# A new memory layout for an FNet block with a gate: x, P, Q and W2 on the 256-byte grid, first tokens staged in the combining buffer

## The chip, the cores and the metric

The kernel runs on one core of one Trainium2 chip. The metric is the device time of one execution in microseconds (us). The kernel before took 714.79 us (median of 3 runs, 714.57 to 714.8). All data are float32; TensorE is fed in the format fp32r (float32 rounded for one pass), so that each product is made from several passes, as told below.

## The reference

With x of 2048 tokens by 512 features (one batch), two 2048 x 2048 and two 512 x 512 DFT matrices, w1 of 512 x 1792 and w2 of 1792 x 512:

```python
xn = layernorm(x)                                   # over features, eps 1e-5
a  = einsum("bsd,ed->bse", xn, dft_hid_re)
b  = einsum("bsd,ed->bse", xn, dft_hid_im)
y  = einsum("ts,bse->bte", dft_seq_re, a) - einsum("ts,bse->bte", dft_seq_im, b)
h  = relu(xn @ w1 + b1) ** 2
out = x + y * silu(h @ w2 + b2)
```

## The kernel before, in words

**Three passes.** Every float32 operand is split into a high part (ScalarE copies it with rounding, `split_hi` L68) and a low part (VectorE subtracts, `split_lo` L71). A product is HI·HI + HI·LO + LO·HI (`PASSES`), three matmuls into one PSUM bank.

**Seven products for eight.** Most products are 2 x 2 block products in seven multiplications (`PRODUCTS`, `ORDER`), with sums of blocks of the one operand (`sums_a`), of the other (`sums_b`) and of the results (`combine`). `A11` to `S4` and `B11` to `T4` name the blocks and sums. A matmul of this kind has 128 x 128 weights and 256 moving columns; each weight load precedes its matmul and runs beside the one before it.

**The stages, in the order of the span** (times in us of the profiled execution):

1. 0 to 112: x is normalised, split and laid down in eight buffers `XC[j]` of 7 blocks x (HI, LO) x 256 floats. The first two chunks (c = 0, 1) of the sequence DFT are done without the seven-product scheme (`products`, L340; 512 moving columns from g1a/g1b, weights from XC). In chunk 1 the sums of x and the splits of the 512 x 512 DFT matrices (`wd_split`, into wd0 and wd1) are made beside it.
2. 112 to 414: chunks c = 2 to 7. Each has 8 steps j; a step is 7 products x 6 matmuls (`mm`, L287): moving operand g0/g1 (`moving`, the split sums of the raw DFT rows that `load_c` brings into `r`), weights `XC[j]`. At a chunk's end the results are combined in `e` and split into P and Q (`pq`, tiles pq00 to pq11). Behind steps 1 and 2 of the next chunk follow the two calls of `stage2` (L273), which multiply P and Q with the feature DFT: 24 passes each, weights from pq, 512 moving columns from wd0/wd1; some of the passes are split into two halves of 256 columns. The result y goes to DRAM. W1 and W2 are also prepared here (`make_w`), written to DRAM.
3. 414 to 564: hidden layer, 28 units (4 token groups c x 7 pairs of 256 hidden features p), 42 matmuls each (L527): weights W1[p], moving operand xT[c, q], the transposed normalised tokens. The two `stage2` calls of chunk 7 follow unit 0. Results are squared and go to DRAM (`HD`).
4. 564 to 706: output product, again 28 units of 42 matmuls (L581): weights are the reloaded, summed and split hidden features g (`operand`, `ready`), moving operand W2[p]. Then silu, times y, plus x, and out. In the last token group the products of the last three p are done product by product, so that the end can start early.

**What sets the order.** Stage 1 for c = 0, and everything from the hidden units on, are written out by hand (`manual_schedule`): `plan` and `go` name what is issued ahead of and behind each unit: `m` loads the rows of mean and 1/deviation, `x` a half token group (`xt_half`), `w` a late W2 block, `h` a step of `operand` (reload, sums, split), `l` a load of a W2 block (`load_w2`, L480). The rest, stages 1 (c = 1) and 2, is ordered by the planner from its own time estimates; DMA loads go through SP's queue.

**Buffers.** SBUF tiles with one tag share a place in turn. The eight x buffers xc0 to xc7 are tiles of 14336 bytes per partition each. They are given new contents later: xc0, xc1 take xT of even token groups and then W2's p = 0, 1; xc2 to xc7 take W1's p = 0 to 5, xc4 to xc6 then g, xc7, xc2, xc3 W2's p = 2, 3, 4. wd0 and wd1 take xT of odd groups and then W2's p = 5, 6. W1's p = 6 lies in g0b and g1b. The first group's tokens are staged, at the steps j = 2 and 3 of chunk 7, in new tiles with the tags xc2 and xc3 (`stage{q}`, L675).

**Remainders.** Tiles lie one behind the other in the order in which their tags are first used, each rounded up to 32 bytes. Counting the sizes gives each tile's address modulo 256. The eight x buffers begin at 3840 and are 56 x 256 bytes long: remainder 0. Behind them the tile `gap` (L113) takes 192 bytes, and the tiles that follow (pq, r, g0, g1, wd, t, e, sx) all have multiples of 256 bytes, or are made such by what precedes them: remainder 192. Blocks inside a tile are multiples of 512 bytes apart, so that an operand has its tile's remainder.

Of the kernel before, what the change touches and what calls it, by code (L numbers as in the profile page):

```python
# [12 lines left out]
P = 128  # L13
# [7 lines left out]
WARM = 8, 5  # L21
PLAIN = 2
# [39 lines left out]
def fnet_gated_kernel(ctx, tc, x, xt, ct, wd, w1, w2, b1, b2, out):  # L62
# [201 lines left out]
    def stage2(c, t, tag="bc"):  # L264
        ps = bank(tag, f"yps{c}_{t}")[:, 0]
        for m in range(2):
            for k in range(ND):
                w = (k % 2) * CW + t * P
                for a_, b_ in PASSES:
                    last = (a_, b_) == (LO, HI) and (m, k) == (1, ND - 1)  # L270
                    pair = (a_, b_) != (HI, HI) and (m, k) in ((0, 1), (1, ND - 1))[t:]
                    for s in (slice(0, 256), slice(256, 512)) if pair else (slice(0, 512),):
                        nc.tensor.matmul(ps[:, s], PQ[c, m, k // 2][:, a_, w:w + P], WD[m, k][:, b_, s],  # L273
                                         start=(m, k) == (0, 0) and (a_, b_) == (HI, HI), stop=last,
                                         skip_group_check=True)
# [200 lines left out]
    W2_HOME = "xc0", "xc1", "xc7", "xc2", "xc3", "wd0", "wd1"  # L476

    def load_w2(p):
        t = W2[p] = buf(W2_HOME[p], [P, 2, 7, 256], f"w2_{p}", F32R)
        nc.sync.dma_start(t.bitcast(F32), W2D[p])  # L480
# [62 lines left out]
    def operand(n, c, p):  # L543
# [18 lines left out]
        g = ready[c, p] = buf(("xc4", "xc5", "xc6")[n % 3], [P, 2, 7, 256], f"g{c}_{p}", F32R)  # L562
# [86 lines left out]
    for c, j in steps:  # L649
# [88 lines left out]
    plan(c, 4, ["l2", "h2"], ["h1"])  # L738
    plan(c, 5, ["h4"], ["h1"])
# [174 lines left out]
```

## Time and profile before

| | |
|---|---|
| time, median of 3 runs | 714.79 us |
| profiled execution: time / span | 714.79 / 713.0 us |
| 0 to 112.24 (layer norm, chunks 0 and 1) | 112.24 us |
| 112.24 to 414.02 (six chunks, twelve stage 2 calls) | 301.78 us |
| 414.02 to 564.45 (hidden units, two stage 2 calls) | 150.43 us |
| 564.45 to 669.43 (output product, groups 0 to 2) | 104.98 us |
| 669.43 to 713.0 (last group, end) | 43.57 us |

The stage borders are the starts of PE's first matmul of a stage. PE is TensorE's matmul unit, PEld its weight load, DVE VectorE, ACT ScalarE, POOL GpSimd, SP the queue that issues most DMAs. In a row of groups, `x42` counts instructions, and "us" is the time from the start of the first to the end of the last. Matmuls overlap by a part of their length, so that the pace of PE is the time from start to start, and not the duration of one (about 280 ns for 256 columns). PEclk is the clock that the throttle granted, 1.00 being full speed. In a window row each engine has its busy time and, in brackets, its number of instructions.

### The profile page before, as it was taken

The numbers are of one execution on the slowest core, as the hardware profiler recorded it, in microseconds if no ns is written. First come the engines' busy times: TensorE is split into PE (matmuls) and PEld (weight loads), VectorE is DVE, ScalarE is ACT, GpSimd is POOL, SyncE is SP. The second block draws the span as 40 slices with busy tenths as digits, with TensorE's granted clock in tenths as the row PEclk, the third lists the DMA queues.
The fourth block names the chain that finished last, engine by engine and source line by source line (L and its number), as shares of the span: only waits on it lengthen the run. The fifth ranks groups of instructions, "written<-read, shape, count | busy, mean of one in ns | idle before, by whom it ended". The sixth has DMA issues, their size and how long they took to land.

```text
span 713.0 us, 12788 instructions
## 1 busy us (share of the span) xinstructions
PE 699.1 (98%) x5197; PEld 662.0 (93%) x5197; DVE 584.8 (82%) x886; ACT 347.1 (49%) x475; POOL 5.2 (1%) x8
## 2 busy tenths in 40 slices
PE   8999999999999999999999999999999999999996
PEld 5778788999999999999999999999999999999995
DVE  7999654779598698797795955999988989989895
ACT  4437333444453544444442424777667764454541
POOL 0000000000000000000000000000000000101000
PEclk9999999999999999999999999999999999999999
DMA  9622531634564653844825669966725996667643
GB/s 325 221 89 90 170 117 39 221 95 143 200 216 133 218 190 125 281 148 151 296 90 160 227 234 350 351 241 207 265 105 190 357 397 196 184 214 201 218 149 113
DMA packets 55020, 141.11 MB, mean 198 GB/s; under 512 B 5041, under 2 KB 21681, under 8 KB 53681
## 3 DMA queue, kind: packets, MB, share of 16 engines
q1 hardware_dynamic: 49840, 124.56, 51.3%
q10 hardware_dynamic: 4032, 14.68, 5.3%
q0 software_dynamic: 1088, 1.05, 1.0%
q8 instruction: 41, 0.67, 0.4%
q14 instruction: 19, 0.15, 0.1%
HBM read 97.00 MB, written 43.27 MB: 197 GB/s over the span
## 4 chain that ended last, share of the span: by engine, by line
PE 83%; DVE 13%; issue 2%; ACT 1%; DMA 0%; DVEq 0%; ACTq 0%
PE m_b L287 24%; PE yps L273 12%; PE m_b_o L581 10%; PE hps L527 9%; PE hps_b L527 5%; PE m_bb L287 5%; PE m_ba L287 5%; DVE g L71 3%; PE pq_b L340 3%; PE hps_ba L527 3%; DVE xc L71 2%; PE m_bc_o L581 1%; DVE bn L128 1%; PE m_ba_o L581 1%; PE m_bb_o L581 1%
## 5 line engine op out<-in xcount | busy, mean ns | idle before, releaser
L287 PE MATMUL m_b<-g,xc 128*128 128x256 f32 x1440 | 179.2, 280 | 0.0
L287 PEld LDWEIGHTS m_b<-g,xc 128*128 128x128 f32 x1440 | 173.3, 189 | 0.4
L71 DVE TENSOR_TENSOR g<-r,g 128x768 fp32r<-128x768 f32 (+2 forms) x65 | 65.5, 1007 | 42.0 <-ACT g L68 41.7
L68 ACT ACTIVATE g<-r 128x768 fp32r<-128x768 f32 (+2 forms) x65 | 57.4, 886 | 84.7 <-PE m_b L287 43.9
L273 PE MATMUL yps<-wd,pq 128*128 128x512 f32 (+1 forms) x432 | 93.2, 366 | 0.0
L273 PEld LDWEIGHTS yps<-wd,pq 128*128 128x128 f32 x432 | 75.8, 188 | 13.4
L581 PE MATMUL m_b_o<-w,g 128*128 128x256 f32 x630 | 78.5, 281 | 0.5 <-ACT m_b_o L574 0.5
L581 PEld LDWEIGHTS m_b_o<-w,g 128*128 128x128 f32 x630 | 76.0, 191 | 0.7 <-ACT m_b_o L574 0.7
L340 PE MATMUL pq_b<-g,xc 128*128 128x512 f32 x240 | 64.7, 399 | 3.9 <-ACT xc L68 2.1
L71 DVE TENSOR_TENSOR g<-t,g 128x1024 fp32r<-128x1024 f32 x48 | 58.6, 1222 | 12.1 <-ACT g L68 12.0
L527 PE MATMUL hps<-xT,w 128*128 128x256 f32 x504 | 61.9, 282 | 0.0
L527 PEld LDWEIGHTS hps<-xT,w 128*128 128x128 f32 x504 | 60.8, 190 | 0.0
L340 PEld LDWEIGHTS pq_b<-g,xc 128*128 128x128 f32 x240 | 43.9, 188 | 17.5 <-ACT xc L68 3.6
L68 ACT ACTIVATE g<-t 128x1024 fp32r<-128x1024 f32 x48 | 50.3, 1048 | 17.0 <-PE m_ba L287 6.5
L538 ACT ACTIVATE h<-h,b1s 128x512 f32<-128x512 f32 x56 | 37.3, 715 | 17.6 <-DVE h L237 17.5
L68 ACT ACTIVATE g<-hr 128x768 fp32r<-128x768 f32 (+1 forms) x28 | 35.5, 1269 | 20.9 <-PE m_ba_o L581 5.3
L71 DVE TENSOR_TENSOR g<-hr,g 128x768 fp32r<-128x768 f32 (+1 forms) x28 | 41.6, 1485 | 2.3 <-ACT g L68 2.2
L287 PE MATMUL m_bb<-g,xc 128*128 128x256 f32 x288 | 42.7, 280 | 0.0
L287 PE MATMUL m_ba<-g,xc 128*128 128x256 f32 x288 | 42.5, 280 | 0.0
L287 PEld LDWEIGHTS m_bb<-g,xc 128*128 128x128 f32 x288 | 37.8, 189 | 0.3
L287 PEld LDWEIGHTS m_ba<-g,xc 128*128 128x128 f32 x288 | 37.5, 189 | 0.0
L196 DVE TENSOR_TENSOR t<-r 128x512 f32<-128x512 f32 x48 | 32.9, 685 | 5.2 <-DMA r<-in_ct 5.0
(172 smaller groups left out, 1004.0 us busy)
## 6 DMA issues: line engine op xcount, KB each, us to landing
r<-in_ct SPq DMA_DIRECT2D x63, 512.0 KB, 3.7
hd<-h ACTq DMA_DIRECT2D x28, 512.0 KB, 4.5
hr<-hd SPq DMA_DIRECT2D x28, 512.0 KB, 4.6
w1d<-w0g SPq DMA_DIRECT2D x21, 512.0 KB, 3.5
w<-w1d SPq DMA_DIRECT2D x6, 1792.0 KB, 9.2
w<-w2d SPq DMA_DIRECT2D x4, 1792.0 KB, 12.0
y<-ysb SPq DMA_DIRECT2D x16, 256.0 KB, 3.2
fin<-y SPq DMA_DIRECT2D x16, 256.0 KB, 5.2
```

The lines of the kernel that those rows point to most:

```text
L68: nc.scalar.activation(hi, src, AF.Copy)
L71: return nc.vector.tensor_tensor(lo, src, hi.bitcast(F32), op=ALU.subtract)
L128: nc.vector.bn_stats(bn, t[:, h])
L196: nc.vector.tensor_tensor(t[:, 0:2], r[:, 0:1].to_broadcast([P, 2, 256]), r[:, 1:3], op=ALU.add)
L273: nc.tensor.matmul(ps[:, s], PQ[c, m, k // 2][:, a_, w:w + P], WD[m, k][:, b_, s], start=(m, k) == (0, 0) and (a_, b_) == (HI, HI), stop=last,
L287: nc.tensor.matmul(ps[:, d * CW:(d + 1) * CW], w[:, a_, d * P:(d + 1) * P], mv(b_), start=first and d == 0 and (a_, b_) == (HI, HI), stop= ...
L340: nc.tensor.matmul(accs[c][k], w, g[:, b_, 2 * h:2 * h + 2], start=j == 0 and h == 0 and (a_, b_) == (HI, HI), stop=j == NJ - 1 and h == 1 ...
L527: nc.tensor.matmul(product(ms, k), W1[p][a][:, a_, q * P:(q + 1) * P], xT[c, q][:, b_, b], start=share not in first, stop=q == 1 and (a_, ...
L538: nc.scalar.activation(x_[:, s], x_[:, s], AF.Relu, bias=b1s[:, f:f + 1])
L581: nc.tensor.matmul(m[:, k * 256:(k + 1) * 256], g[:, a_, a, k * P:(k + 1) * P], W2[p][:, b_, b], start=p == 0 and k == 0 and (a_, b_) == ( ...
```

## The change

`LINE` is 16 floats, 64 bytes.

- The order of the tiles is written down: xc0, xc1, the four pq tiles, wd0, wd1, then one tile `block` for the other six x buffers with 64 spare bytes, then the small `stats_t`, g0a, g1a, g0b, g1b, b1s and eps, and the rest as it comes. The tile `gap` and the small tiles laid down ahead of time (`few`) are gone.
- x buffer j from 2 to 7 is a slice of `block`, from the top down (`sixth`): the x data with offset 0, W1's p = 0 to 5 and g at the same places with an offset of 64 bytes, W2's p = 2, 3, 4 in the places of j = 5, 6, 7 with offset 0. A slice with the offset overlaps by 64 bytes with the one above it.
- By the same count, xc0, xc1, pq, wd and `block` now have the remainder 0; g0 and g1 192; r 32; t, e and sx 64.

| product (line) | moving, weights before | moving, weights after |
|---|---|---|
| chunks 0, 1 (L340), chunks 2 to 7 (L287) | 192, 0 | 192, 0 |
| stage 2 (L273) | 192, 192 | 0, 0 |
| hidden, p < 6, even / odd c (L527) | 0, 0 / 192, 0 | 0, 64 |
| hidden, p = 6, even / odd c | 0, 192 / 192, 192 | 0, 192 |
| output, p = 0 to 4 / 5, 6 (L581) | 0, 0 / 192, 0 | 0, 64 |

- `stage2` writes its passes as a list of 24 and splits other ones in halves. Before, in the first call of a chunk passes 4, 5, 22, 23 (counted from 0) were split, in the second 22 and 23. Now pass 23 is split in every call but the last of all, and in the first call of chunks before 7 passes 4 and 5 too; in the last call of all pass 1 is split and its second half is done at the very end.
- The first group's tokens are staged in `e` (the rows, and the raw first half), in an r and in t tiles, in steps: load at j = 2 and 4, the rest at j = 3 and 6. W1's first loads stay at j = 4 to 7.
- The load of W2's p = 2 (`l2`) is issued at unit (3, 5) of the hidden layer instead of (3, 4).

```diff
+LINE = 16
...
-    small = {tag: [buf(tag, [P, n], f"{tag}_{i}", bufs=3) for i in range(3)] for tag, n in (("bn", 12), ("sm", 4))}
...
-    XC = [buf(f"xc{j}", [P, 7, 2, 256], f"xc{j}", F32R) for j in range(NJ)]
-
-    pool.tile([P, 48], F32, name="gap")
+    for tag, n in [("xc0", 3584), ("xc1", 3584)] + [(f"pq{m}", 1024) for m in ("00", "01", "10", "11")] \
+            + [("wd0", 4096), ("wd1", 4096)]:
+        buf(tag, [P, n], f"place_{tag}")
+    block = pool.tile([P, 6 * 3584 + LINE], F32R, name="block")
+    stats_t = pool.tile([P, 2 * NS], F32, name="stats_t")
+    for tag, n in (("g0a", 1536), ("g1a", 2048), ("g0b", 1536), ("g1b", 2048)):
+        buf(tag, [P, n], f"place_{tag}")
...
+    def sixth(j, a, on=LINE):
+
+        v = block[:, (7 - j) * 3584 + on:][:, 0:3584]
+        return v.rearrange("p (a b n) -> p a b n", a=a, n=256)
+
+    XC = [buf(f"xc{j}", [P, 7, 2, 256], f"xc{j}", F32R) if j < 2 else sixth(j, 7, 0) for j in range(NJ)]
...
     def stage2(c, t, tag="bc"):
         ps = bank(tag, f"yps{c}_{t}")[:, 0]
...
+        whole, one, two = slice(0, 512), slice(0, 256), slice(256, 512)
+        todo = [(m, k, a_, b_, whole) for m in range(2) for k in range(ND) for a_, b_ in PASSES]
+
+        def divide(n):
+            todo[n:n + 1] = [(*todo[n][:4], half) for half in (one, two)]
+
+        if (c, t) == (NC - 1, 1):
+            divide(1)
+            todo.append(todo.pop(2))
+        else:
+            divide(23)
+        if c < NC - 1 and t == 0:
+            divide(5)
+            divide(4)
...
-            t = buf(f"xc{2 + (p + 2) % 6}", [P, 2, 7, 256], f"w1_{p}", F32R)
+            t = sixth(2 + p, 2)
...
-    W2_HOME = "xc0", "xc1", "xc7", "xc2", "xc3", "wd0", "wd1"
+    W2_HOME = "xc0", "xc1", 5, 6, 7, "wd0", "wd1"
...
-        t = W2[p] = buf(W2_HOME[p], [P, 2, 7, 256], f"w2_{p}", F32R)
+        to = W2_HOME[p]
+        t = W2[p] = sixth(to, 2, 0) if p in (2, 3, 4) else buf(to, [P, 2, 7, 256], f"w2_{p}", F32R)
...
-        g = ready[c, p] = buf(("xc4", "xc5", "xc6")[n % 3], [P, 2, 7, 256], f"g{c}_{p}", F32R)
+        g = ready[c, p] = sixth(2 + n % 3, 2)
...
-            if j in (2, 3):
-                q = j - 2
-                t = buf(f"xc{2 + q}", [P, 3, 4, 256], f"stage{q}")
-                if q == 0:
-                    load_rows(0, t[:, 0])
-                list(xt_half(0, q, lambda k: t[:, 1 if k == "r" else 2]))
-            elif j > 3:
+            if j == 2:
+                e = buf("e", [P, 8, 256], "rows0")
+                load_rows(0, e[:, 0:4])
+            if j in (2, 4):
+                first = xt_half(0, j // 2 - 1, lambda k: e[:, 4:8] if (j, k) == (2, "r") else
+                                buf(k, [P, 4, 256], f"x{k}0", bufs=3 if k == "r" else 2))
+                next(first)
+            if j in (3, 6):
+                list(first)
+            if j > 3:
                 load_w1(j - 4)
...
-    plan(c, 4, ["l2", "h2"], ["h1"])
-    plan(c, 5, ["h4"], ["h1"])
+    plan(c, 4, ["h2"], ["h1"])
+    plan(c, 5, ["l2", "h4"], ["h1"])
```

More of the change, by code (lines that the diff above doesn't have):

```diff
@@ L79, in fnet_gated_kernel @@
     dram = ctx.enter_context(tc.tile_pool(name="dram", bufs=1, space=bass.MemoryType.DRAM))
-    b1s = pool.tile([P, NF], F32, name="b1s")
     b2s = pool.tile([P, D], F32, name="b2s")
-    eps = pool.tile([P, 1], F32, name="eps")
     stats = pool.tile([P, 2, 2, NJ], F32, name="stats")
-    stats_t = pool.tile([P, 2 * NS], F32, name="stats_t")
     rows = dram.tile([2 * NS, P], F32, name="rows")
     Y = [dram.tile([TC, D], F32, name=f"y{t}") for t in range(NTC)]
-    nc.vector.memset(eps, EPS)
     def bank(tag, name):
@@ L96, in buf @@
         return pool.tile(shape, dtype, tag=tag, bufs=bufs, name=name)
-    small = {tag: [buf(tag, [P, n], f"{tag}_{i}", bufs=3) for i in range(3)] for tag, n in (("bn", 12), ("sm", 4))}
-    def few(tag, n, name):
-        return small[tag].pop(0) if small[tag] else buf(tag, [P, n], name, bufs=3)
     def bcast(src, n):
@@ L108, in halves @@
         return ap.rearrange("p (a b) -> p a b", a=2)
-    XC = [buf(f"xc{j}", [P, 7, 2, 256], f"xc{j}", F32R) for j in range(NJ)]
-    pool.tile([P, 48], F32, name="gap")
+    for tag, n in [("xc0", 3584), ("xc1", 3584)] + [(f"pq{m}", 1024) for m in ("00", "01", "10", "11")] \
[5 more added lines that the diff above has]
+        buf(tag, [P, n], f"place_{tag}")
+    b1s = pool.tile([P, NF], F32, name="b1s")
+    eps = pool.tile([P, 1], F32, name="eps")
+    nc.vector.memset(eps, EPS)
+    def sixth(j, a, on=LINE):
+        v = block[:, (7 - j) * 3584 + on:][:, 0:3584]
+        return v.rearrange("p (a b n) -> p a b n", a=a, n=256)
+    XC = [buf(f"xc{j}", [P, 7, 2, 256], f"xc{j}", F32R) if j < 2 else sixth(j, 7, 0) for j in range(NJ)]
     xr, xn32 = {}, {}
@@ L124, in ln_stats @@
         t = xr[j]
-        sm = few("bn", 12, f"bn{j}_{hs.start}")
+        sm = buf("bn", [P, 12], f"bn{j}_{hs.start}", bufs=3)
         for h in range(hs.start, hs.stop):
@@ L134, in ln_root @@
         n = hs.stop - hs.start
-        t = root[j] = few("sm", 4, f"root{j}_{hs.start}")
+        t = root[j] = buf("sm", [P, 4], f"root{j}_{hs.start}", bufs=3)
         nc.scalar.activation(t[:, 0:n], stats[:, 1, hs, j], AF.Sqrt, bias=eps)
@@ L265, in stage2 @@
         ps = bank(tag, f"yps{c}_{t}")[:, 0]
[L266 to L275, printed above, removed]
+        whole, one, two = slice(0, 512), slice(0, 256), slice(256, 512)
[10 more added lines that the diff above has]
+            divide(4)
+        for n, (m, k, a_, b_, s) in enumerate(todo):
+            w = (k % 2) * CW + t * P
+            nc.tensor.matmul(ps[:, s], PQ[c, m, k // 2][:, a_, w:w + P], WD[m, k][:, b_, s],
+                             start=n == 0, stop=n > len(todo) - 3, skip_group_check=True)
         if t == 0:
```

## The prediction

> **What bounds the kernel now.** I read the page's first section, then the windows cut at the stage borders, then PE's timeline inside each stage for the pace of its matmuls, and last the waits of PE and of SP's queue.
>
> ```profile
> PE 699.1 (98%) x5197; PEld 662.0 (93%) x5197; DVE 584.8 (82%) x886; ACT 347.1 (49%) x475; POOL 5.2 (1%) x8
> ...
> core 0: 713.0 us, clock 0.998
> ```
> ```profile
> core 0: us, PE busy (x) PEld busy (x) DVE busy (x) ACT busy (x) POOL busy (x), PEclk, DMA share, GB/s
> 112.24:414.02 301.78, 301.78 (x2342) 291.52 (x2341) 237.53 (x352) 132.30 (x179) 0.00 (x0) 1.00 0.52 175
> 414.02:564.45 150.43, 150.43 (x1232) 148.72 (x1231) 126.18 (x184) 97.16 (x136) 0.00 (x0) 1.00 0.69 250
> 564.45:669.43 104.98, 104.52 (x884) 104.25 (x884) 95.38 (x126) 54.11 (x61) 4.99 (x4) 1.00 0.73 241
> ```
>
> PE is busy 98% of the span at full granted clock. From 112.24 to 414.02 (six chunks of the L287 product with twelve calls of stage 2) and from there to 564.45 (28 hidden units, two calls of stage 2) it is never idle; in the first three token groups of the output product it idles 0.46 us. So nothing but the time from one matmul's start to the next can shorten these 557 us. That time is not one number. I take it as the difference of two neighbouring starts, over the count of the first row:
>
> ```profile
> 440.06 5.20 PE L527 MATMUL hps<-xT,w 128*128 128x256 f32 x42
> 445.10 0.88 PE L527 MATMUL hps_bb<-xT,w 128*128 128x256 f32 x6
> ```
> ```profile
> 457.22 2.20 PE L527 MATMUL hps_b<-xT,w1b 128*128 128x256 f32 x18
> 459.26 0.84 PE L527 MATMUL hps_b<-xT,w1a 128*128 128x256 f32 x6
> ```
> ```profile
> 479.73 5.11 PE L527 MATMUL hps<-xT,w 128*128 128x256 f32 x42
> 484.68 0.87 PE L527 MATMUL hps_bb<-xT,w 128*128 128x256 f32 x6
> ```
> ```profile
> 491.07 3.04 PE L527 MATMUL hps<-xT,w1b 128*128 128x256 f32 x24
> 493.95 0.88 PE L527 MATMUL hps<-xT,w1a 128*128 128x256 f32 x6
> ```
>
> One line of code, one shape, yet 5.04/42 = 120.0 ns, 2.04/18 = 113.3, 4.95/42 = 117.9 and 2.88/24 = 120.0. What differs is where the two operands lie. Counted from the tiles' sizes, the big x buffers sit on the 256-byte grid (remainder 0), and the 192-byte tile `gap` puts all later tiles on remainder 192. Written (moving, weights), the four pairs are (0,0), (0,192), (192,0) and (192,192): equal remainders give 120.0, (0,192) gives 113.3, (192,0) here 117.9. But (192,0) has a second pace:
>
> ```profile
> 586.08 3.76 PE L581 MATMUL m_b_o<-w,g 128*128 128x256 f32 x30
> 589.68 0.88 PE L581 MATMUL m_ba_o<-w,g 128*128 128x256 f32 x6
> 590.40 0.86 PE L581 MATMUL m_bb_o<-w,g 128*128 128x256 f32 x6
> 591.10 3.56 PE L581 MATMUL m_b_o<-w,g 128*128 128x256 f32 x30
> 594.50 0.84 PE L581 MATMUL m_ba_o<-w,g 128*128 128x256 f32 x6
> ```
> ```profile
> 217.07 4.36 PE L287 MATMUL m_b<-g,xc 128*128 128x256 f32 x37
> 221.26 0.84 PE L287 MATMUL m_ba<-g,xc 128*128 128x256 f32 x6
> ```
> ```profile
> 248.91 3.70 PE L287 MATMUL m_b<-g,xc 128*128 128x256 f32 x30
> 252.44 0.87 PE L287 MATMUL m_ba<-g,xc 128*128 128x256 f32 x6
> ```
>
> In the output product, p = 4 is (0,0) at 3.60/30 = 120.0; then p = 5 is (192,0), and after six matmuls at 116.7 it runs at 3.40/30 = 113.3. In L287, all (192,0), 4.19/37 = 113.2 stands beside 3.53/30 = 117.7: the same addresses hold either pace for long, and what ran just before chooses. Behind a (0,0) stretch the trace shows 113.3; behind a whole call of stage 2, which is (192,192) now, mostly 117.7.
>
> **The change part by part.** Counted the same way, the new layout leaves L287 at (192,0), puts stage 2 from (192,192) to (0,0), the hidden units from (0,0) or (192,0) to (0,64) for p < 6 and to (0,192) for p = 6, and the output product, (0,0) for p ≤ 4 and (192,0) for p = 5, 6, to (0,64) throughout. L340's products stay at (192,0).
>
> *Stage 2.*
>
> ```profile
> 232.83 5.65 PE L273 MATMUL yps<-wd,pq 128*128 128x512 f32 x26
> 238.31 0.87 PE L287 MATMUL m_bb<-g,xc 128*128 128x256 f32 x6
> ```
> ```profile
> 109.37 2.26 PE L340 MATMUL pq_b<-g,xc 128*128 128x512 f32 x9
> 111.47 0.86 PE L340 MATMUL pq_ba<-g,xc 128*128 128x512 f32 x3
> ```
>
> A call of 24 passes takes 5.48 us (228 ns a pass) at (192,192); 512 columns at (192,0) take 2.10/9 = 233.3. At (0,0) no row has 512 columns. As 256 columns pace alike at (0,0) and (192,192), I take 228: zero, with 233.3 as the upper bound, 384 passes × 5 ns = +2 us. Below zero there is little: twice 113.3 is 226.7, so at most −0.5. Passes split in halves cost nothing by themselves (two halves at 113.3 are one pass); there are fewer of them, and their places decide how the stream enters what follows.
>
> *L287 chunks.* 301.78 less 12 × 5.48 leaves 236.0 us for 2016 matmuls (6 × 8 × 42), 117.1 on average: most at 117.7, some at 113.3. With stage 2 at (0,0) the entry into (192,0) is that of the output product's p = 4 to 5, so I take 113.3 everywhere: 228.4, a gain of 7.6; two entries a chunk at six times 3.4 ns are 0.2, and I leave 0.3 more for passes that the scheduler mixes among the matmuls: −7.1. Ends: −7.6, and +1.3 if all 2016 run at 117.7.
>
> *Hidden units.* 150.43 less 2 × 5.48 is 139.5 us for 1176 matmuls, 118.6 each. The (0,64) of the new layout appears nowhere in the trace. Its nearest rows are those with unequal remainders and the moving operand on the grid, (0,192) at 113.3, and unequal remainders generally, 113.3 or 117.7, against 120.0 for equal ones. I take 113.3: 133.2, −6.3. DVE then has to be as fast: 126.18 busy less its share of the stage border, in 144 us instead of 150. That holds on average; for places where it is late I give back 0.8: −5.5. Ends: −6.3 and, at 117.7, −1.1.
>
> *Output product, groups 0 to 2.* 882 matmuls at 113.3 are 99.9; the 0.46 us of idle time stays, and 0.5 for DVE (95.38 busy of 101): 100.9, −4.1. Ends −5.0 and (117.7) −0.7.
>
> *Last group and tail.*
>
> ```profile
> 669.43:691.96 22.53, 21.31 (x177) 21.02 (x175) 22.01 (x29) 11.14 (x13) 0.00 (x0) 1.00 0.51 166
> 691.96:713.00 21.04, 13.91 (x118) 13.71 (x118) 13.57 (x23) 3.25 (x7) 0.00 (x0) 0.95 0.42 141
> ...
> PE m L581 <- DVE g L71: 1.3, 1, 1.3
> ```
>
> Up to 691.96 DVE is busy 22.01 of 22.53 and PE ends by waiting 1.3 us for DVE's g: a faster PE only waits longer, 0. Behind it 118 matmuls gain up to 0.6; of that 0.4 is on the path.
>
> *DVE and ACT on moved buffers.*
>
> ```profile
> L71 DVE TENSOR_TENSOR xT<-xt,xT x2: 1216/1222/1227, 445.5 to 459.0; 128x1024 fp32r<-128x1024 f32 x2
> ...
> L71 DVE TENSOR_TENSOR xT<-xt,xT x2: 1217/1217/1217, 479.5 to 493.1; 128x1024 fp32r<-128x1024 f32 x2
> ```
>
> The same split writes to remainder 192 in the first row (group 1) and to 0 in the second (group 2): 1222 and 1217 ns. DVE doesn't see the grid; 0.
>
> *W2's third block, one unit later.*
>
> ```profile
> 549.64 0.33 SPq L480 DMA_DIRECT2D w<-w2d  x1
> 575.28 0.88 PE L581 MATMUL m_bb_o<-w,g 128*128 128x256 f32 x6
> ...
> SPq L480 <- PE hps_b L527: 9.3, 1, 9.3
> ...
> w<-w2d SPq DMA_DIRECT2D x4, 1792.0 KB, 12.0
> ```
>
> Its new place overlaps 64 bytes of W1's p = 4, so it is issued behind unit (3,4) instead of (3,3): about 5.0 us (42 × 120.0) after 549.64, landing 12.0 later at about 567, 8 us ahead of its first use at 575.28. While SP waits for it, the reloads h4 and those of the next unit queue behind; the 9.3 us that SP waits now show that the queue bears that. Cost 0; were the landing 8 us later, that much would be paid by PE at p = 2.
>
> *First tokens through `e`, t and r.* The same DMAs, sums and splits as before, issued at j = 2 to 6 of the last chunk instead of 2 and 3.
>
> ```profile
> 363.72:414.02 50.30, 50.30 (x392) 48.59 (x391) 40.02 (x54) 19.88 (x25) 0.00 (x0) 1.00 0.54 173
> ```
>
> DVE has 10.3 us free in that chunk. It loses about 1 us of it to the faster PE; a wait on t's two buffers would delay the moving sums of the chunk, which run two steps ahead (12 us of PE). 0. W1's first loads go to buffers read two steps earlier than now, so SP waits less there; nobody waits for them now. The small tiles' new order: 0.
>
> Sum: −7.1 − 5.5 − 4.1 − 0.4 = −17.1; 713.0 − 17.1 = 695.9, and 1.79 us outside the span (the profiled execution took 714.79, the median itself) make **697.7**.
>
> **The rivals.**
> *Only one of hidden and output product gets 113.3* (DVE binds in the other, or its entry falls to the slow pace): 714.8 − 12.6 = 702.2 without the output product, 703.2 without the hidden units. For it: DVE would be busy 88 to 95% there.
> *(0,64) runs at 117.7*: −7.1 − 1.1 − 0.7 = 706. For it: a remainder of 64 has no row at all.
> *L287 stays at 117.7 behind stage 2*: +1.3 − 10.0 = 706.1. For it: an entry from a 512-column stretch at (0,0) isn't shown, only from 256 columns.
> *Both*: +1.3 − 1.8 = 714.3, no change.
> *Addresses decide nothing*, and the paces come from something else that goes with the stages. The rows against it are the four pairs of L527: same code, same shapes. Then 714.8. [...]
> *Slower: stage 2 on the grid doesn't lock.* Its passes then take 233.3 (+2 us) and leave L287 at 117.7 (+1.3), while (0,64) turns out no better than equal remainders (hidden and output as now, +0): 718. It decides from a pace of 231 ns a pass.
> *Slower: the one tile `block` is ordered as a whole*, so that W1's loads wait for the last read of any x at 414 and each of the 28 g for all reads before it: a load (12.0) and 28 splits of the 1.2 us shown for xT lie bare, +46 − 17, 743. It decides at the first idle time of PE behind 414. Against it: buffers are already shared in slices by the loads of x.
>
> **How the numbers follow.** Forecast 0.45 (its own range 694.5 to 701.5: all ends fast make −19.8, DVE and entries costing twice as much −14); one of two 0.17; (0,64) slow 0.12; L287 slow 0.08; both 0.06; addresses nothing 0.03; stage 2 not locking 0.06; block as a whole 0.03. Range 694.5 to 708, which leaves out the last four (0.18). A measurement tells some 0.2%, 1.4 us, from no change: faster 0.82, same 0.09, slower 0.09.
>
> **What would show it.** Right: starts 113.3 ns apart in L287 behind both stage 2 calls, in L527 at p < 6 and in L581 at every p; the windows of chunks near 49.1 us, seven hidden units near 33.5 and seven output units near 33.6 us; DVE's waits on PE gone and PE's waits on DVE g in their place, by a few us at most. Wrong: 117.7 or 120.0 in any of these, a stage 2 call over 5.55 us, a wait of PE for w<-w2d, or idle time at 414.

## The result and the profile after

The changed kernel takes **710.56 us** (median of 4 runs, 709.39 to 711.26) against 714.79: ratio 0.9939, 95% interval 0.9922 to 0.9957. It is faster, as forecast, but by 4 us instead of 17, and lies outside the range. The profiled execution took 710.93.

The profile after, its first section, the span, and the windows cut at the same stage borders (columns as before: length, then busy time and count of each engine, clock, DMA):

```profile
PE 687.0 (97%) x5179; PEld 647.7 (91%) x5179; DVE 584.5 (82%) x886; ACT 347.3 (49%) x475; POOL 5.2 (1%) x8
...
core 0: 709.1 us, clock 0.995
```
```profile
112.03:406.84 294.81, 294.81 (x2330) 284.23 (x2328) 237.00 (x352) 132.28 (x179) 0.00 (x0) 1.00 0.53 189
406.84:558.54 151.70, 147.19 (x1228) 144.66 (x1227) 125.95 (x184) 96.27 (x134) 0.00 (x0) 1.00 0.58 217
558.54:664.03 105.49, 101.60 (x885) 100.77 (x883) 95.90 (x127) 54.99 (x62) 4.99 (x4) 1.00 0.75 253
664.03:686.70 22.67, 20.39 (x178) 20.00 (x176) 22.15 (x29) 11.20 (x13) 0.00 (x0) 1.00 0.53 179
686.70:709.10 22.40, 15.29 (x118) 15.09 (x118) 13.45 (x23) 3.22 (x6) 0.00 (x0) 0.84 0.40 133
```

| stage | before | after | change | forecast |
|---|---|---|---|---|
| 0 to the chunks' first matmul | 112.24 | 112.03 | −0.2 | 0 |
| six chunks with stage 2 | 301.78 | 294.81 | −7.0 | −7.1 |
| hidden units | 150.43 | 151.70 | +1.3 | −5.5 |
| output groups 0 to 2 | 104.98 | 105.49 | +0.5 | −4.1 |
| last group up to PE's wait | 22.53 | 22.67 | +0.1 | 0 |
| end | 21.04 | 22.40 | +1.4 | −0.4 |

(The borders used for the kernel before lie 0.07 to 0.08 us behind the first matmuls, which start at 112.17, 413.94, 564.38 and 669.35; the stages' lengths don't change by it.) PE is busy 12 us less than before (687.0 for 699.1), and the span is only 4 us shorter: the rest became idle time, of which the windows show 4.5 us in the hidden stage and 3.9 in the output product, where there was 0 and 0.5. What PE waited for (total, times, longest):

```profile
PE hps_bb L541 <- DMA block<-w1d: 3.0, 1, 3.0
PE m L595 <- DVE block L72: 2.3, 1, 2.3
PE m_b_o L595 <- ACT m_b_o L588: 2.3, 3, 1.3
...
PE m_bb_o L595 <- DMA w<-w2d: 1.6, 1, 1.6
PE hps_ba L541 <- DMA w1b<-w1d: 1.5, 1, 1.5
```

The loads of W1 and W2, for which PE did not wait before, hold it up three times. The pace came out as forecast in the chunks, and behind them in most places. In the lines of the changed kernel L300 is the chunks' product (L287 before), L287 is stage 2 (L273), L541 the hidden layer (L527) and L595 the output product (L581). From PE's timeline, behind the second stage 2 call of a chunk, then two places of the hidden stage (start, length, count):

```profile
230.25 5.62 PE L287 MATMUL yps<-wd,pq 128*128 128x512 f32 x25
235.71 0.86 PE L300 MATMUL m_bb<-g,block 128*128 128x256 f32 x6
236.41 3.56 PE L300 MATMUL m_b<-g,block 128*128 128x256 f32 x30
239.81 0.84 PE L300 MATMUL m_ba<-g,block 128*128 128x256 f32 x6
...
429.73 2.88 PE L541 MATMUL hps_b<-xT,block 128*128 128x256 f32 x24
432.45 4.92 PE L541 MATMUL hps<-xT,block 128*128 128x256 f32 x42
...
477.06 5.11 PE L541 MATMUL hps<-xT,block 128*128 128x256 f32 x42
482.00 0.87 PE L541 MATMUL hps_bb<-xT,block 128*128 128x256 f32 x6
```

The stage 2 call takes 5.46 us, the chunks' product behind it 3.40/30 = 113.3 ns where it took 117.7, and the new (0,64) 2.72/24 = 113.3 in one place and 4.94/42 = 117.6 in another, the whole of token group 1. So (0,64) has the same two paces as (192,0), 113.2 and 117.7 in the kernel before.

**Why W1's p = 4 came late.** SP's timeline and PE's around the last stage 2 call; after:

```profile
411.94 11.15 PE L287 MATMUL yps<-wd,pq 128*128 128x512 f32 x50
422.93 4.92 PE L541 MATMUL hps<-xT,block 128*128 128x256 f32 x42
...
423.12 1.75 SPq L312 DMA_DIRECT2D rows<-rows  x4
427.36 2.46 SPq L480 DMA_DIRECT2D block<-w1d  x2
...
SPq L312 <- PE yps L287: 14.6, 1, 14.6
```

and before:

```profile
418.98 11.18 PE L273 MATMUL yps<-wd,pq 128*128 128x512 f32 x54
429.99 2.19 PE L527 MATMUL hps<-xT,w 128*128 128x256 f32 x17
...
426.09 1.75 SPq L299 DMA_DIRECT2D rows<-rows  x4
431.54 1.67 SPq L467 DMA_DIRECT2D w<-w1d  x2
```

The rows of the next token group are loaded into the tag pq00. Before, they were issued 3.9 us ahead of the end of stage 2, now 0.2 us behind it. Everything behind them on SP's queue moves with them: W1's p = 4 and 5 are issued 4.4 us after the end of stage 2 instead of 1.6, and unit 4 needs p = 4 a little earlier than before. In the code there is one reason: `todo.append(todo.pop(2))` puts the second half of pass 1 of the very last call at the very end, and pass 1 (m = 0, k = 0) reads its weights from pq00.

### The profile page after: what moved, and what is told of

It is laid out like the page before. It is cut to its first block, busy times and chain, and to the rows that moved or that the text cites. A ratio compares the mean times of both kernels' runs of the same rounds, so it can differ in the third digit from the quotient of the medians.

```text
span 709.1 us, 12790 instructions
## 1 busy us (share of the span) xinstructions
PE 687.0 (97%) x5179; PEld 647.7 (91%) x5179; DVE 584.5 (82%) x886; ACT 347.3 (49%) x475; POOL 5.2 (1%) x8
## 3 DMA queue, kind: packets, MB, share of 16 engines
q0 software_dynamic: 1088, 1.05, 1.0%
## 4 chain that ended last, share of the span: by engine, by line
PE 73%; DVE 16%; DMA 6%; issue 2%; ACT 2%; SPq 0%; DVEq 0%; ACTq 0%
PE m_b L300 23%; PE yps L287 12%; PE hps L541 7%; PE m_b_o L595 7%; PE m_bb L300 5%; PE m_ba L300 5%; PE hps_b L541 4%; DVE block L72 4%; PE pq_b L353 3%; DMA w1b<-w1d 3%; PE hps_ba L541 2%; DVE g L72 2%; DMA w2raw<-in_w 2%; PE m_bc_o L595 1%; DMA xr<-in_xt 1%
## 5 line engine op out<-in xcount | busy, mean ns | idle before, releaser
L300 PE MATMUL m_b<-g,block 128*128 128x256 f32 x1080 | 129.0, 276 | 0.0
L300 PEld LDWEIGHTS m_b<-g,block 128*128 128x128 f32 x1080 | 125.5, 188 | 0.0
L287 PE MATMUL yps<-wd,pq 128*128 128x512 f32 (+1 forms) x414 | 92.9, 374 | 0.0
L287 PEld LDWEIGHTS yps<-wd,pq 128*128 128x128 f32 x414 | 74.8, 188 | 14.0
L541 PE MATMUL hps<-xT,block 128*128 128x256 f32 x504 | 59.9, 278 | 0.0
L541 PEld LDWEIGHTS hps<-xT,block 128*128 128x128 f32 x504 | 58.7, 188 | 0.2
L353 PE MATMUL pq_b<-g,block 128*128 128x512 f32 x180 | 47.6, 398 | 1.8 <-DVE g L72 1.7
L595 PE MATMUL m_b_o<-w,block 128*128 128x256 f32 x360 | 44.0, 278 | 2.3 <-ACT m_b_o L588 2.3
L300 PE MATMUL m_b<-g,xc 128*128 128x256 f32 x360 | 45.1, 277 | 0.0
L595 PEld LDWEIGHTS m_b_o<-w,block 128*128 128x128 f32 x360 | 42.2, 188 | 2.9 <-ACT m_b_o L588 2.9
L69 ACT ACTIVATE block<-hr 128x768 fp32r<-128x768 f32 (+1 forms) x28 | 35.5, 1268 | 18.4 <-DVE hr L209 9.3
L300 PEld LDWEIGHTS m_b<-g,xc 128*128 128x128 f32 x360 | 42.9, 188 | 0.3
L72 DVE TENSOR_TENSOR block<-hr,block 128x768 fp32r<-128x768 f32 (+1 forms) x28 | 41.6, 1485 | 0.9 <-ACT block L69 0.8
L541 PE MATMUL hps_b<-xT,block 128*128 128x256 f32 x288 | 35.1, 278 | 0.0
L541 PEld LDWEIGHTS hps_b<-xT,block 128*128 128x128 f32 x288 | 34.1, 188 | 0.0
```

Of the source, the lines that this page charges most:

```text
L69: nc.scalar.activation(hi, src, AF.Copy)
L72: return nc.vector.tensor_tensor(lo, src, hi.bitcast(F32), op=ALU.subtract)
L300: nc.tensor.matmul(ps[:, d * CW:(d + 1) * CW], w[:, a_, d * P:(d + 1) * P], mv(b_), start=first and d == 0 and (a_, b_) == (HI, HI), stop= ...
L353: nc.tensor.matmul(accs[c][k], w, g[:, b_, 2 * h:2 * h + 2], start=j == 0 and h == 0 and (a_, b_) == (HI, HI), stop=j == NJ - 1 and h == 1 ...
L541: nc.tensor.matmul(product(ms, k), W1[p][a][:, a_, q * P:(q + 1) * P], xT[c, q][:, b_, b], start=share not in first, stop=q == 1 and (a_, ...
L595: nc.tensor.matmul(m[:, k * 256:(k + 1) * 256], g[:, a_, a, k * P:(k + 1) * P], W2[p][:, b_, b], start=p == 0 and k == 0 and (a_, b_) == ( ...
```

## The experiments

My theory for the result: the addresses decide the pace as I said, and two edits that I had costed at nothing hold back loads on SP's queue, the half pass that keeps pq00 and W2's p = 2 placed behind h2's reload. The rivals: the places of the halves, not the addresses, make the chunks faster; the loads are late because DMA is full, whatever their order; DVE bounds what follows.

Stage times are those of one profiled execution each; hidden stage and output groups 0 to 2 are taken from the first matmul of the stage to the first of the next. The chunks took 294.8 to 295.1 us in every kernel of this table. The ratio compares a kernel with the kernel before, run beside it on the same chip; the rows come from several chips, so that rows are compared by their ratios. The profiled execution was the fastest of its kernel's in e1_half, e3_splits, e6_pass19, e9_w2line and e11_order_only, and the slowest in e12_less_dma. The kernels marked * don't compute the reference's output, as told with each.

| kernel | median us | ratio to before, 95% | hidden | groups 0 to 2 |
|---|---|---|---|---|
| the change | 710.56 | 0.9939 (0.9922 to 0.9957) | 151.7 | 105.5 |
| e1_half | 707.48 | 0.9884 (0.9863 to 0.9906) | 146.5 | 105.6 |
| e2_line0 | 717.63 | 1.0034 (1.0021 to 1.0048) | 156.5 | 108.4 |
| e3_splits | 707.03 | 0.9891 (0.9875 to 0.9908) | 145.8 | 105.7 |
| e4_grid | 712.03 | 0.9955 (0.9941 to 0.9970) | 153.0 | 106.7 |
| e5_l2 * | 709.61 | 0.9920 (0.9906 to 0.9934) | 156.2 | 101.3 |
| e6_pass19 | 707.80 | 0.9906 (0.9891 to 0.9921) | 149.1 | 105.5 |
| e7_both * | 708.48 | 0.9904 (0.9888 to 0.9920) | 154.0 | 103.6 |
| e8_line48 * | 714.17 | 0.9985 (0.9975 to 0.9996) | 156.7 | 104.8 |
| e9_w2line | 705.00 | 0.9870 (0.9853 to 0.9888) | 145.3 | 104.2 |
| e10_order | 706.18 | 0.9878 (0.9863 to 0.9892) | 145.6 | 106.3 |
| e11_order_only | 710.00 | 0.9933 (0.9918 to 0.9948) | 150.8 | 106.3 |
| e12_less_dma * | 705.01 | 0.9860 (0.9830 to 0.9890) | 150.3 | 103.1 |
| e13_less_dve * | 705.72 | 0.9862 (0.9828 to 0.9897) | 146.6 | 106.8 |
| e14_w2line2 | 705.28 | 0.9854 (0.9828 to 0.9880) | 147.4 | 103.6 |

### e1_half: the half pass back in its place

```diff
-        if (c, t) == (NC - 1, 1):
-            divide(1)
-            todo.append(todo.pop(2))
-        else:
-            divide(23)
+        divide(23)
```

> The changed kernel with the last stage 2 call written like the others (its pass 23 in halves; the second half of pass 1 no longer comes last), so that pq00 is read for the last time a quarter into that call. Theory (the moved half holds pq00 until the end of stage 2; the rows' loads wait for it on SP's queue, and W1's p = 4, 5, 6 queue behind them): the rows are issued some 4 us before stage 2 ends, W1's p = 4 near 423 us instead of 427, PE waits for no W1 block, the hidden stage takes 146 to 148 us instead of 151.7, and the time is 704 to 707. Rival (DMA is simply full there and the faster PE gets ahead of it, whatever SP's order): a wait of 3 us or more for W1 stays, hidden stage over 150, time 709 to 711.

SP's and PE's timeline of e1_half:

```profile
419.42 1.74 SPq L308 DMA_DIRECT2D rows<-rows  x4
424.84 1.62 SPq L476 DMA_DIRECT2D block<-w1d  x2
...
423.31 5.11 PE L537 MATMUL hps<-xT,block 128*128 128x256 f32 x42
428.26 0.87 PE L537 MATMUL hps_bb<-xT,block 128*128 128x256 f32 x6
```

The rows go out 3.9 us ahead of the end of stage 2 (423.31) again, W1's p = 4 1.5 us behind it, and the only wait left in the hidden stage is 0.5 us. Hidden stage 146.5 and profile 704.66, as the theory had it; the median, 707.5, is 0.5 above its range. The queue, not a full DMA by itself, made the wait. But group 0 now runs at 4.95/42 = 117.9. Ending stage 2 on whole pairs of halves led into the slow pace (117.9 in e1) in all three such profiles with (0,64) (e1, e3, e5), and ending it on a single half into the fast one (113.6 in e6) in all nine (the change, e6, e7, e9 to e14).

### e2_line0: the offset of 64 bytes taken away

```diff
-    def sixth(j, a, on=LINE):
+    def sixth(j, a, on=0):
```

> The changed kernel with W1's blocks and g at offset 0 instead of 64 bytes in their places (same tiles, 64 bytes unused): hidden p < 6 and the output product become (0,0). Theory: 120.0 ns in both, chunks as in the changed kernel (294.8 us), the wait for W1's p = 4 shrinks to about 2 us, hidden stage 152 to 153, output groups 35 or more each; time 711 to 713. Rival (what the offset gains on PE is all given back to DVE and DMA): no slower than the changed kernel, 710.6 or less.

717.63, slower than the kernel before, and 7 us slower than the change. Nothing but this offset moves in it, so it is the cleanest test of the addresses. The chunks keep their gain (294.8); hidden and output run at 120.0 throughout except p = 6 of the hidden layer, (0,192), which takes 113.3 from group 1 on. I had the direction and not the size: group 0 of the hidden stage waits 4.3 us in four places, not 2. So the offset is worth 7 us net of all that DVE and DMA take back, and without it the change would be a loss.

### e3_splits: the halves of stage 2 as before

```diff
-        if (c, t) == (NC - 1, 1):
-            divide(1)
-            todo.append(todo.pop(2))
-        else:
-            divide(23)
-        if c < NC - 1 and t == 0:
+        divide(23)
+        divide(22)
+        if t == 0:
```

> The changed kernel with the split halves of stage 2 as before (passes 4, 5, 22, 23 in a chunk's first call, 22, 23 in the second, none moved). Theory (the addresses alone choose the pace): L287 at 113.3 behind every call, chunks 294.5 to 295.5 us, and as the moved half is gone too, the rest as with that half put back: 704 to 707. Rival (the places of the halves choose the pace): L287 falls to 117.7 behind the calls, chunks 299 to 302, time 710 to 713.

Chunks 295.0, their product at 113.6 on average, hidden stage 145.8, time 707.03. The places of the halves don't matter to the chunks; with pq00 free early the hidden stage comes out as in e1_half.

### e4_grid: only stage 2's operands on the grid

```diff
-    pool.tile([P, 48], F32, name="gap")
+    for tag, n in [(f"pq{m}", 1024) for m in ("00", "01", "10", "11")] + [("wd0", 4096), ("wd1", 4096)]:
+        buf(tag, [P, n], f"place_{tag}")
+    pool.tile([P, 48], F32, name="gap")
```

> The kernel before with one thing changed: the pq and wd tiles lie ahead of the 192-byte gap, so that stage 2 is (0,0) instead of (192,192); xT of odd groups and W2's p = 5, 6, which lie in wd, go to remainder 0 as well. Splits, staging and loads as before. Theory (the entry from a (0,0) stretch gives 113.3): chunks 294.8 to 295.5 us instead of 301.8; hidden p < 6 of odd groups from 117.8 to 120.0, +1.2 us; output p = 5, 6 from 113.3 to 120.0, +1.7 to +2.4; time 710 to 711.5. Rival (the new places of the halves, or 64-byte offsets, are needed): chunks stay at 301 to 302, time 717 to 719.

Chunks 295.1, 6.7 us less than before, from this edit alone: moving P, Q and the feature DFT weights from remainder 192 to 0 makes the chunks' matmuls between them faster (113.7 ns on average for 116.9), whose own remainders are unchanged. (The edit puts pq and wd ahead of r, g0 and g1, so that these move too, by multiples of 256 bytes; that this matters nothing isn't shown apart.) Hidden odd groups rise to 120.0, p = 5 and 6 of the output too; 712.03, 0.5 above the expectation, with 1.3 us of waits in the hidden stage that the kernel before didn't have.

### e5_l2, e7_both: W2's p = 2 early; e6_pass19: another half pass last

e6 and e7 put the second half of pass 19 last, which reads pq11; e5 is built on e1_half. e5 and e7 have the load back at unit (3,4).

```diff
-            divide(1)
-            todo.append(todo.pop(2))
+            divide(19)
+            todo.append(todo.pop(20))
...
-    plan(c, 4, ["h2"], ["h1"])
-    plan(c, 5, ["l2", "h4"], ["h1"])
+    plan(c, 4, ["l2", "h2"], ["h1"])
+    plan(c, 5, ["h4"], ["h1"])
```

> The kernel of e1_half with the load of W2's p = 2 put back ahead of h2's reload at unit (3,4), as before. Theory (behind h2's reload on SP the load starts 7 us later against the end of the hidden layer, the W2 loads then pile up with the reloads in a full DMA, and DVE and PE wait for hr, w2raw and w): it is issued some 14 us ahead of the output product instead of 7.7, output group 0 takes 35 to 35.8 us instead of 36.8, groups 0 and 1 together 69 to 70.5 instead of 72.1; time 2 to 3 us below e1_half. Rival (DVE alone bounds the output product, so that earlier data only turn into later waits for DVE): groups 0 to 2 together stay within 0.7 us of e1_half's 105.6, same time within 1 us.

> The changed kernel with another pass put last in the last stage 2 call: the second half of pass 19, which reads pq11 like the passes around it, instead of pass 1, which reads pq00. So the stream ends on a half as in the changed kernel, but pq00 comes free early. Theory (the wait came from pq00 alone, and ending on one half is what lets the hidden units enter 113.3): no wait for W1's p = 4, units 1 to 5 at 113.3 instead of e1_half's 117.8, hidden stage 145 to 146 us instead of 146.5; time 1 to 2 below e1_half. Rival (the pace after stage 2 comes from something else): units 1 to 5 at 117.8, time as e1_half.

> e6_pass19 with the load of W2's p = 2 back at unit (3,4). Theory (both costs add): 3 to 4.5 us below e1_half, 703 to 704.5, and hidden stage 145 to 146, output groups 0 and 1 below 70.5 together. Rival (DVE bounds what is left): what the hidden stage gains comes back as waits for DVE in the output product, time within 1 us of e1_half.

e6_pass19, PE's timeline behind stage 2:

```profile
423.17 4.93 PE L541 MATMUL hps<-xT,block 128*128 128x256 f32 x42
427.94 0.84 PE L541 MATMUL hps_bb<-xT,block 128*128 128x256 f32 x6
```

4.77/42 = 113.6 where e1_half has 117.9, and no wait for p = 4: the stream enters fast behind one half, and pq00 was the whole reason of the wait for p = 4. The time is no better than e1_half's all the same: in the profiled execution PE waits 2.6 us at unit 6 for W1's p = 6 (0.5 in e1_half) and then runs at half its clock for 3.4 us (granted 0.63 and 0.94 in the two windows of 4 us from 450 to 458: 2.96 + 0.48). That needn't be so: e9, e10, e12, e13 and e14 have the same order up to there, and wait 0.2, 0.6, 2.6, 1.6 and 2.5 us at the same place, since the load lands at different times (451.04 in e6, 448.92 in e10). The hidden stage of e10 takes 145.6, what I had expected of e6.

In e5, e7 and e8 the early load overwrites the last 64 bytes (192 in e8) of W1's p = 4 before unit (3,4) reads them, so that their output isn't the reference's. The unit also has to wait for that load, 5.5 us in e5 and e7 and 4.8 in e8, so the times of e5 and e7 answer nothing. e5's output groups take 101.3 us, near the 100.9 that I had forecast for the change; but the 5.5 us wait gave DMA and DVE time to get ahead (not shown apart), so e5 doesn't show what the early load alone is worth. e9_w2line is the clean version.

### e8_line48: 192 bytes instead of 64

```diff
-LINE = 16
+LINE = 48
...
-    stats_t = pool.tile([P, 2 * NS], F32, name="stats_t")
     for tag, n in (("g0a", 1536), ("g1a", 2048), ("g0b", 1536), ("g1b", 2048)):
         buf(tag, [P, n], f"place_{tag}")
+    stats_t = pool.tile([P, 2 * NS], F32, name="stats_t")
```

> e7_both with the offset of W1's blocks and g at 192 bytes instead of 64 (the small stats_t moves behind g1b, so that g0 and g1 keep remainder 192): hidden and output product are all (0,192). Theory (any unequal remainder gives 113.3 or 117.7, chosen by what ran before): same time as e7_both within 1 us, 117.7 still seen after a wait of PE. Rival (moving on 0 with weights on 192 has the fast pace only, as p = 6 showed before): no matmul at 117.7 in hidden and output, up to 2 us less PE time there.

Built on e7_both, and 5.7 us slower in the same series: nearly every matmul of hidden and output at 117.8 (a token group without waits 34.63 us instead of 33.32). Both sides were wrong, the theory in the time, the rival in the pace. (0,192), which I had only seen at 113.3, holds 117.8 for most of 250 us, entered in the same way as e7's (0,64).

### e9_w2line, e10_order, e11_order_only, e14_w2line2: the W2 load without a clash

```diff
-        t = W2[p] = sixth(to, 2, 0) if p in (2, 3, 4) else buf(to, [P, 2, 7, 256], f"w2_{p}", F32R)
+        t = W2[p] = sixth(to, 2, LINE if p == 2 else 0) if p in (2, 3, 4) else buf(to, [P, 2, 7, 256], f"w2_{p}", F32R)
```

That is e9, beside e7's two edits; e14 has `LINE if p < 4` and l3 at unit (3,5). e10 (on e6) and e11 (on the change) have only this order:

```diff
-    plan(c, 4, ["h2"], ["h1"])
-    plan(c, 5, ["l2", "h4"], ["h1"])
+    plan(c, 4, [], ["h1", "l2", "h2"])
+    plan(c, 5, ["h4"], ["h1"])
```

> e7_both with W2's p = 2 also at offset 64, in exactly the place of W1's p = 3, so that its early load touches nothing of W1's p = 4 (in e5, e7 and e8 it overwrites 64 bytes of that block before unit (3,4) reads it, and the unit waits 5 us for the load). Theory (two costs, both of SP's order, are gone; the output units p = 2 become (64,64), four at 120.0, +1.1 us): hidden stage 145 to 146 us, output groups 0 to 2 102 to 103 together, no wait for a W1 or W2 block over 1 us, time 701 to 704. Rival (DVE bounds the output product): groups 0 to 2 at 105 or more, time 706 or more.

> e6_pass19 with the order of two loads exchanged: W2's p = 2 (at offset 0, as in the changed kernel) is issued behind unit (3,4) and ahead of h2's reload, which comes behind it. Theory (the load was late because h2's reload, which waits for the buffer e, stood ahead of it on SP): it starts about 13 to 14 us ahead of the output product less the 4.8 of one unit, near -9.5 instead of -7.7; groups 0 to 2 together 102.5 to 104.5, time 702.5 to 705.5. Rival (only a start as early as before helps): groups 0 to 2 at 105 to 106, as the changed kernel.

> The changed kernel with the order of the two loads exchanged as in e10_order and nothing else, so that pass 1 still ends stage 2. Theory: hidden stage 150.5 to 152 with the wait for W1's p = 4, output groups 0 to 2 as in e10_order, time 707.5 to 709.5. Rival: no gain, 710 to 711.

> e9_w2line with W2's p = 3 treated alike: at offset 64 in the place of W1's p = 4, loaded at unit (3,5) instead of (3,6). Four more output units become (64,64), +1.1 us, and the load starts about one unit earlier. Theory (the two prices are about equal): 700 to 703 in the profile and the same median as e9_w2line within 1 us, group 0 at 34.5 to 35.3. Rival (the DMA is no longer full after p = 2 alone): 1 us slower than e9_w2line.

In the change, h2's reload and behind it the load of W2's p = 2 on SP's queue:

```profile
550.42 0.33 SPq L566 DMA_DIRECT2D hr<-hd  x1
550.84 0.39 SPq L494 DMA_DIRECT2D block<-w2d  x1
...
SPq L566 <- DVE w L72: 11.2, 1, 11.2
```

In e9_w2line the load, and the hidden stage and groups 0 to 2:

```profile
538.39 0.33 SPq L494 DMA_DIRECT2D block<-w2d  x1
...
407.18:552.48 145.30, 145.05 (x1229) 142.86 (x1227) 125.68 (x184) 95.95 (x134) 0.00 (x0) 1.00 0.64 236
552.48:656.72 104.24, 102.05 (x885) 101.39 (x883) 95.86 (x127) 55.00 (x62) 4.99 (x4) 1.00 0.74 244
```

The load starts 14.1 us ahead of the output product (552.48) instead of 7.7 (558.54), PE waits for no block over 0.2 us, and the hidden stage takes the forecast 145. The groups take 104.2, above the 102 to 103 expected; 0.8 of it is the price of their three units at (64,64) (3.60/30 = 120.0 there, so 42 × 6.7 ns each; the fourth such unit is in the last group). The median, 705.0, is 1 us above my range. e9's ratio of 0.9870 can't be told from those of e14, e10 and e1_half, whose intervals overlap with its own. e14 has the same median, as expected, but its group 0 (35.5 us) and its profile (705.28) missed their ranges. One place earlier in the order, with the start 10.0 us ahead of the output product (e10 and e11), gained nothing in the groups: there the rival was right.

e10 and e11 differ only in the half that ends stage 2, so they are also the cleanest test of pq00: with pass 1 last (e11) the hidden stage takes 150.8, with waits of 3.1 and 1.8 us for W1's p = 4 and 6, with pass 19 last (e10) 145.6, with 0.6 for p = 6 alone. The ratios are 0.9933 and 0.9878.

### e12_less_dma, e13_less_dve: what bounds group 0

```diff
+        if p in (3, 4):
+            W2[p] = W2[2]
+            return
         nc.sync.dma_start(t.bitcast(F32), W2D[p])
```

> e6_pass19 without two loads: W2's p = 3 and 4 aren't loaded, the product reads p = 2's block for all three (the output isn't the reference's), so that 3.6 MB are missing just ahead of and in output group 0; DVE's work is the same. Theory (the full DMA delays hr, w2raw and W2, DVE sits idle for them, falls behind and PE with it): group 0 at 34 to 35 us instead of 37.2, DVE's waits for DMA in it under 1 us instead of 5, groups 0 to 2 together 101 to 102.5 instead of 105.5. Rival (DVE's own work is the bound): groups 0 to 2 at 104.5 or more.

> e6_pass19 without the multiplication by y of output groups 0 to 2 (12 DVE instructions of 0.69 us, run in groups 1 to 3; the output isn't the reference's), transfers as they were. Theory (DMA delays group 0; DVE only makes the delay last because it has no slack to catch up): group 0 stays at 36.5 to 37.3 us, group 1 falls from 34.8 to 33.4 to 34.2 us, groups 0 to 2 together by 0.5 to 1.3; PE's wait for g in the last group (2.3 us) falls by 1 to 2 us. Rival (DVE's work is the bound from the start): group 0 falls too, groups 0 to 2 at 103 or less.

e13 leaves out both lines `times(c, e, k)` of `finish`. DVE's waits around output group 0 in e6_pass19, then in e12_less_dma:

```profile
DVE w2raw L201 <- DMA w2raw<-in_w: 3.2, 1, 3.2
DVE hs L207 <- DMA hr<-hd: 1.3, 1, 1.3
DVE block L72 <- ACT block L69: 0.8, 1, 0.8
DVE hr L207 <- DMA hr<-hd: 0.6, 1, 0.6
```
```profile
DVE hs L207 <- DMA hr<-hd: 1.1, 1, 1.1
DVE block L72 <- ACT block L69: 0.9, 1, 0.9
```

Without the two W2 loads group 0 falls from 37.2 to 35.0 us and DVE's waits for DMA from 5.1 to 1.1; in the seven kernels at offset 64 that start the load of W2's p = 2 at most 10 us ahead of the output product, group 0 takes 36.8 to 37.6. (Group 1 happened to run at 117.8, +1.3, so the sum is 103.1 and not 102.) Without the multiplications group 0 stays at 36.8, and PE's wait for g in the last group falls from 2.35 to 0.2 us. So DMA sets group 0; that DVE, which has little slack behind it, carries the delay to the end fits the wait for g that e13 takes away. The forecast for e13's group 1 failed: it took 36.5, at 117.8 and with 1.4 us of waits for ACT's bias, and groups 0 to 2 together rose to 106.8 where a fall was expected.

## Why the prediction was wrong, point by point

- **Chunks, −7.1: right**, −7.0. Stage 2 at (0,0) lets (192,0) run at 113.3; e4 shows that the places of stage 2's operands do it without the rest of the change, e3 that the halves don't. By the rival in which addresses decide nothing, the layout gains nothing; 6.7 us in the chunks of e4 speak against that, and so do the 7 us of e2.
- **Hidden units, −5.5: the pace was right in size, the step that failed is another.** With the waits gone the stage takes 145.3 (e9) against my 144.9. That this is so near is in part luck: the 0.8 that I gave back was for a late DVE, for which PE never waits there; slow stretches of group 0 and a 0.2 us wait for p = 6 took it instead. The failed step is the sentence that passes split in halves "cost nothing by themselves", and that "their places decide how the stream enters what follows". It left out what the half that is moved to the end reads. pq00 stays taken, the rows wait for it on SP, and W1's p = 4 behind them arrives 3.0 us late; between e11 and e10 this one half is worth 5.2 us of the stage. How much of the 1.5 us wait for p = 6 belongs to it isn't shown, since kernels with pq00 free wait there too (0 to 2.6 us). The moved half did bring what I had only supposed of the places: the fast entry (e1_half against e6_pass19, 117.9 and 113.6). Behind the two waits group 1 ran at 117.6, 1.3 us more, but it need not: e11, with the same code up to there and the same two waits, runs it at 113.3 (4.76/42):

```profile
457.79 4.92 PE L541 MATMUL hps<-xT,block 128*128 128x256 f32 x42
462.55 0.84 PE L541 MATMUL hps_bb<-xT,block 128*128 128x256 f32 x6
```

- **"I take 113.3" for (0,64): half right.** It runs there for most of the time, but has 117.8 as well. The nearest row that I chose it by, (0,192) at 113.3, was too short a stretch to show its second pace (e8). What chooses between the two at entry, beyond single cases, stays open.
- **W2's third block, cost 0: wrong.** I took the start as 5 us later and asked only whether its own landing is in time. It was: PE never waits for p = 2. But h2's reload now stands ahead of it and waits 11.2 us for `e`, which holds a raw W2 block until DVE has split it; the load starts 7 us later against the end of the hidden stage, and what it displaces is the rest of a full DMA (share 1.00 to 1.02 in the windows from 552 to 582): reloads and the raw block of p = 6, for which DVE waits 2.1 and 3.2 us, and the block of p = 5, for which PE waits 1.6 us. Of the 4.6 us by which groups 0 to 2 missed the forecast, an early start brings back 2.1 without the price of the (64,64) units (e9 against the change: 1.25 + 0.84). Of the remainder, the traces show 2.2 us of waits for ACT's bias in e9 (0.5 before); in the change two of the three such waits (0.62 and 0.33 us) stand behind waits of ACT for DVE's z, 2.05 us each. That the faster PE meets a DMA that was full before the change too (share 0.95 to 1.05 from 551 to 582) is what e12 suggests, and not shown apart.
- **Output product, "0.5 for DVE": too small.** DVE's busy time in groups 0 to 2 is 95.9 us of 105.5; what DMA costs DVE in group 0 isn't caught up before the last group, where PE waits 2.3 us for g.
- **Last group, 0: right** (+0.1). **The end, −0.4: wrong**, +1.4. The forecast's "a faster PE only waits longer" left out the clock behind the longer wait (2.3 us for 1.3), 0.50 for a time; below.
- Staging in `e`, r and t, the order of the small tiles, DVE on moved buffers: no cost, as forecast; the last chunk is as long as the others, and DVE's total is 584.5 for 584.8.
- Two sums of the forecast are off by less than 1 us: without the output product it leaves out the 0.4 of the end (701.8 for 702.2), and its own range begins at 694.5 where all ends fast give 695.0. Nothing hangs on them.

## What to carry to other kernels

When PE is busy 98% of the time, compare its start-to-start times between places with the same code: here six per cent at most hung on where two operands lie against each other modulo 256 bytes (120.0 ns at equal remainders, 113.3 or 117.8 at unequal ones), and in single cases the choice between 113.3 and 117.8 on what ran just before (e1_half against e6_pass19). When an instruction is moved later, list the buffers that it reads and who waits to overwrite them; on a queue like SP's here, everything behind that waiter moves as well (W1's p = 4 from 1.6 to 4.4 us behind stage 2). And when a transfer is started later, ask not only whether it lands in time but which transfers it then competes with (group 0 took 37.2 us with W2's p = 3 and 4 among them, 35.0 without).

## What the runs showed of the hardware

**Two paces for one layout.** With unequal remainders, 256-column matmuls run at 113.3 or at 117.8 ns, for hundreds of matmuls at a time, in (192,0), (0,64) and (0,192) alike (the last at 113.3 for 153 at most, in e8); equal ones run at 120.0. The remainders are counted from the sizes; that 256 bytes is the measure that matters isn't shown apart. In these traces the pace mostly changes at a wait or at a matmul of another layout or width (in e1's last group 2.83/24 = 117.9 ahead of the 1.7 us wait and 2.72/24 = 113.3 behind it). A wait need not change it (e11), and in e7, e10, e12 and e13 it goes from 117.8 to 113.3 at the start of output group 2 without any of these; in e12 from 1.42/12 = 118.3 to 3.40/30 = 113.3:

```profile
628.25 1.58 PE L598 MATMUL m_b_o<-w,block 128*128 128x256 f32 x12
629.67 0.87 PE L598 MATMUL m_ba_o<-w,block 128*128 128x256 f32 x6
630.38 2.23 PE L598 MATMUL m_b_o<-w,block 128*128 128x256 f32 x18
...
633.12 3.56 PE L598 MATMUL m_b_o<-w,block 128*128 128x256 f32 x30
636.52 0.84 PE L598 MATMUL m_ba_o<-w,block 128*128 128x256 f32 x6
```

So single executions differ: group 1 of the hidden layer takes 34.6 us in the change and 33.3 in e11 with the same code up to there. e1_half's four runs lie between 704.66 and 707.97, those of the kernel before in the same series between 714.77 and 716.12. How much of that is the pace isn't shown, as one execution of each kernel has a trace, and the mean granted clock differs as well (0.998, 0.994, 0.992 and 0.996 in e1_half).

**Half clock behind a short wait.** The end of the change lost 1.4 us though its matmuls' pace became faster. Windows of the change behind PE's 2.3 us wait for DVE (the column behind the five engines is the granted clock):

```profile
688.00:689.00 1.00, 1.00 (x8) 1.00 (x7) 1.00 (x2) 0.00 (x0) 0.00 (x0) 0.62 0.88 259
689.00:690.00 1.00, 1.00 (x7) 1.00 (x6) 1.00 (x2) 0.00 (x0) 0.00 (x0) 0.50 0.87 279
690.00:691.00 1.00, 1.00 (x6) 1.00 (x6) 0.04 (x1) 0.00 (x0) 0.00 (x0) 0.50 0.98 308
691.00:692.00 1.00, 1.00 (x8) 1.00 (x7) 0.00 (x0) 0.00 (x0) 0.00 (x0) 0.68 1.09 385
```

For some 3.4 us (0.76 + 1 + 1 + 0.64, from the shares) PE has half its clock, which by estimate costs half of that, 1.7 us. From the last group's first matmul to the end the change takes 45.1 us, before 43.7, and the seven kernels with the offset of 64 whose clock stayed full there and that do all of the end's work (e1, e3, e5, e6, e7, e9, e11) 43.5 to 43.9. After 1.3 us of waiting at this place, before, the clock stayed full (1.00 from 689 to 694); after 1.7 us it did too (e1, e3, e5), in e14 it fell after 1.8, and in e9 it stayed full after 2.1 (matmuls at 113.3). After 2.3 to 2.4 us it fell in the change, e8, e10 and e12, and not in e6, e7 and e11 (1.00 in the windows of 4 us). The lowest window of 4 us shows 0.64 in e8, 0.71 in e10, 0.65 in e12 and 0.77 in e14. Nor did it fall behind the 3.0 us wait for W1's p = 4 in the change itself (1.00 from 440.3 to 446), so that the length of the wait alone doesn't decide it. What does isn't shown.
